# A state-space and attention kernel: VectorE exp rewritten and used in 96 bursts instead of 82, the skip product moved from TensorE to VectorE, the second state bank freed by row quarters

## Chip, cores, metric

One core of one Trainium2 chip. The metric is the device time of one execution in microseconds (us), the median of several runs. All runs quoted here were in the fast state, which means that none was over 1.5% above the fastest run of the same kernel. A ratio is the mean time of one kernel's fast runs over the mean of the other kernel's fast runs of the same rounds, so it is not quite the ratio of the medians that stand beside it.

In what follows PE is TensorE's matmuls and PEld its weight loads, DVE is VectorE, ACT is ScalarE, POOL is GpSimd, SP is SyncE, and a trailing q (SPq) is an engine's sequencer, which issues DMAs and waits. A line number such as L1085 is a line of that run's own kernel, so the same code has different numbers in different kernels.

## The reference

Two branches read the same `x` (2048 x 1024, bf16) and are mixed by a gate:

```python
g = sigmoid((x * gate_w).sum(-1, keepdims=True))
# a: a diagonal complex state-space layer
h = Lam_bar * h + (x @ B_bar.T)[t]          # along t, 1024 complex states
a = 2.0 * (hseq @ Cmat.T).real + x * Dskip  # x * Dskip is the "skip product"
# b: attention, 32 heads of 32, softmax over 2048 keys
p = softmax(q @ k.T * 32 ** -0.5); b = (p @ v) @ wo
return g * a + (1 - g) * b
```

## The kernel before

The attention is cut into 512 bursts (8 groups of four heads x 8 query blocks x 8 key blocks). A burst makes two tiles of scores, 128x1024 each, in PSUM, the memory that PE writes its results to. Three such tiles of PSUM rotate. ScalarE takes exp of a tile in one instruction. In some bursts ("VectorE bursts") the second half of the first tile, 128x512, goes to VectorE instead. In the gaps PE does everything else, in chains of matmuls into one PSUM bank: projections of the next head group, the state inputs ("u"), the state outputs ("c", 32 tiles of 128x512), and at the end the output product.

The VectorE burst is five instructions:

```python
self.S.op("act", lambda e: e.activation(t[:, 0, :], ps[:, 2 * s, :], ACT.Exp, scale=SCALE), ...)
self.S.op("dve", lambda e: e.tensor_scalar(xi, ps[:, 2 * s + 1, :], EXP_A, EXP_B, ALU.mult, ALU.add), ...)   # exp_a
self.dx += [... tensor_scalar(hi, hi, 0.0, 128.0, ALU.max, ALU.mult) ...,          # exp_b
            ... scalar_tensor_tensor(xw, lo, EXP_C2, lo, ALU.add, ALU.mult) ...,   # exp_c
            ... scalar_tensor_tensor(xw, xw, EXP_C1, lo, ...) ...,                 # exp_d
            ... scalar_tensor_tensor(t[:, 1, :], xw, EXP_C0, ev, ...) ...]         # exp_f
```

A c tile is 16 matmuls and four small ones for the skip product (`x` block times a diagonal of `Dskip`). VectorE scales the sum into one buffer, `Ag[:, 0]`, and the SP queue stores it:

```python
for q in range(4):
    mms.insert(5 * q + 3, (0, lambda e, f, l, ...: e.matmul(ps[:, 7, 128 * q:128 * (q + 1)],
        xT[:, dt, 128 * tt:128 * (tt + 1)], self.diagD[:, dt, :], start=False, stop=False), ...))
def evac():
    self.dve(lambda e: e.tensor_scalar(a, ps[:, 7, :], self.gcol[:, 0, tt:tt + 1], None, ALU.mult), [("bank", 7), "g0"], [at], "evac_c")
    self.dma(lambda e: e.dma_start(self.agd[tile], a), [at], [("agd", tile)], "st_a")
```

Nearly all DMAs are issued by SP, in the order in which a scheduler recorded them; a DMA that has to wait makes SP wait, and all behind it (7.42 us in the timeline below). What must be waited for is worked out from tokens: who writes a token waits for its last writer and readers. A head group's projection weights are three loads of 256 KB (`part` 1, 2, 0). From group 3 on, their buffer has also been scratch for VectorE bursts, so they write that scratch's tokens as well.

Of the kernel before, what the change touches and what calls it, by code (L numbers as in the profile page):

```python
# [8 lines left out]
I32 = mybir.dt.int32  # L9
# [15 lines left out]
RC_MIN = 1e-10  # L25
RC_MAX = 1e12
# [707 lines left out]
class GpPhaseA:  # L734
# [196 lines left out]
ACT_LAG = 0.466  # L931
# [7 lines left out]
EXP_A = 16713.9646930418  # L939
EXP_B = 4936176.0  # L940
EXP_C2 = 189883.03836007958
EXP_C1 = 38303098318.667244
EXP_C0 = 3607248267949745.0
# [3 lines left out]
    "u2 p2 u4 p1 u2 p2 u2 p9 u8 p1 u1 p1 u1 p1 u1 p1 u1 p1 u1 p1 u1 p1 c1 p2 c1 p2 c1 p1 u4 c1 u2 p1 c1 p2 c1 u2 p4 c1 p2 c1 u2 p3 u2 c2 u1 c6 u1 p12 u4 "  # L947
    "p1 u2 p1 u4 p9 c5 p1 c3 u4 p1 u2 p1 u2 p1 u4 p1 u2 p8 u2 p9 c8 p3 o36 ").split())
DVB_RUNS = ((109, 113), (129, 177), (185, 257), (277, 277), (285, 329), (345, 345), (365, 381), (389, 453), (461, 505))
# [19 lines left out]
class FastPath:  # L969

    def __init__(self, nc, S, es, d, flag):
# [20 lines left out]
        hp = T("hp", [128, 2, 8, 512], BF)  # L992
        self.hpb = [hp, self.OT[:, 4:8, :].rearrange("p (r a) n -> p r (a n)", r=2).rearrange("p r (j t) -> p r j t", j=8)]
# [14 lines left out]
        self.diagD = T("diagD", [128, 8, 128], BF)  # L1008
# [6 lines left out]
        self.badb = T("badb", [128, 2], BF)  # L1015

# [14 lines left out]
        hx = [hp[:, r, 4:8, :].rearrange("p a n -> p (a n)") for r in range(2)]  # L1031
        wx = [self.w[:, x].rearrange("p q a n -> p (q a n)") for x in range(2)]
        ag = self.Ag[:, 1, :]
        self.xt = half(wx[0]) + half(wx[1]) + half(hx[0]) + half(self.OT[:, 6, :]) + [ub[:, 0], ub[:, 1]]
        self.xi = [wx[0][:, 2048:3072], wx[1][:, 2048:3072], hx[1][:, 0:1024], self.OT[:, 7, 0:1024], self.ut[:, 0, :]]
        self.xi = [ap.bitcast(I32) for ap in self.xi]
        self.xw = [ag, ag, hx[1][:, 1024:2048].bitcast(F32), self.OT[:, 7, 1024:2048].bitcast(F32), self.ut[:, 1, :]]
# [56 lines left out]
    def begin(self):  # L1094
        S, d = self.S, self.d
        pool, dve, act = self.pool, self.dve, self.act
        warm = self.hpb[0][:, 0, 0, :]
# [61 lines left out]
    def opening(self):  # L1159
        S, ps, w, xT, dve = self.S, self.ps, self.w, self.xT, self.dve  # L1160

        def evac(dst, bank, tok, first, eng=dve):
            src = ps[:, bank, 0:256]
            kw = dict(reads=[("bank", bank)])
            kw.update(dict(writes=[tok]) if first else dict(acc=[tok]))
            if eng is dve:
                S.op("dve", lambda e: e.tensor_copy(dst, src), name="evac_qk", **kw)
            else:
                S.op("act", lambda e: e.activation(dst, src, ACT.Copy), name="evac_qk", **kw)
        for word in self.OPENING.split():  # L1170
# [44 lines left out]
            elif op == "M":  # L1215
# [7 lines left out]
                self.diag_d()  # L1223
# [86 lines left out]
    def diag_d(self):  # L1310
        for j in range(8):
            self.pool(lambda e, j=j: e.tensor_scalar(self.diagD[:, j, :], self.ident[:], self.pf[:, 3, j:j + 1], 0.0, ALU.mult, ALU.add),
                      ["ident", ("pf", 3)], [("diagD", j)])
# [36 lines left out]
    def item_ops(self, j, ch, n):  # L1350
        dve, ub, tq, ut, ht = self.dve, self.ub, self.tq, self.ut, self.ht
        b = self.hp_of[ch]
        hp = self.hpb[b]
        er, ei = self.Et[:, 0, j, :], self.Et[:, 1, j, :]
# [3 lines left out]
        t = [tq[:, i, :] for i in range(4)]  # L1358
        ops = []
# [17 lines left out]
        late = lambda: []  # L1377
        if ch == 2 and j >= 4:
            late = lambda: self.x_toks(2)
        if b == 1 and j == 0:  # L1380
            hw = ["fX", "fY", "m_c"] + self.EFtok + ["gp%d" % i for i in range(4)]
        tt(0.335, hp[:, 0, j, :], t[0], t[1], ALU.subtract, [("tq", 0)], lambda: [("hp", b, j, 0)] + hw + late())
        tt(0.335, hp[:, 1, j, :], t[2], t[3], ALU.add, [("tq", 2)], lambda: [("hp", b, j, 1)] + hw + late())
        if j == 7 and ch < 3:
            ops.append((0.0, self.carry))
        return ops

# [29 lines left out]
    def d_qk(self, g, part, ch, bank=7):  # L1417
        ps, w, xT = self.ps, self.w, self.xT
        mms = []
        for a in range(8):  # L1420
            mms.append((1, lambda e, f, l, a=a: e.matmul(ps[:, bank, :], w[:, g % 2, part, a, :], xT[:, a, 512 * ch:512 * (ch + 1)], start=f, stop=l),  # L1421
                        [("w", g % 2, part)] + self.xtok(ch)))
        if part == 0:
            z = (4 * g + ch) % 5
            dst, tok = self.Q[:, z, :], ("Q", z)
        else:
            dst, tok = self.K[:, g % 2, 512 * ch:512 * (ch + 1)], ("K", g % 2, ch)
        return self.chain(mms, "proj", lambda: self.dve(lambda e: e.tensor_copy(dst, ps[:, bank, :]), [("bank", bank)], [tok], "evac_qk"), bank)
# [42 lines left out]
    def d_c(self, ch, tq, cb, k):  # L1471
        ps, xT, cT = self.ps, self.xT, self.cT
        b = self.hp_of[ch]
        hp = self.hpb[b]
        tt = 4 * ch + tq
        cols = slice(128 * tq, 128 * (tq + 1))
        mms = []
        for j in range(8):
            for ri in range(2):
                mms.append((1, lambda e, f, l, j=j, ri=ri: e.matmul(ps[:, 7, :], hp[:, ri, j, cols], cT[ri][:, j, 512 * cb:512 * (cb + 1)], start=f, stop=l),  # L1480
                            [("hp", b, j, ri), ("cTf", ri, j)]))


        for q in range(4):
            dt = 4 * cb + q
            mms.insert(5 * q + 3, (0, lambda e, f, l, q=q, dt=dt: e.matmul(ps[:, 7, 128 * q:128 * (q + 1)], xT[:, dt, 128 * tt:128 * (tt + 1)], self.diagD[:, dt, :],  # L1486
                                                                          start=False, stop=False), [("diagD", dt)] + self.xtok(ch)))
# [4 lines left out]
        def evac():  # L1492
            self.dve(lambda e: e.tensor_scalar(a, ps[:, 7, :], self.gcol[:, 0, tt:tt + 1], None, ALU.mult), [("bank", 7), "g0"], [at], "evac_c")
            self.dma(lambda e: e.dma_start(self.agd[tile], a), [at], [("agd", tile)], "st_a")
# [4 lines left out]
    def ld_a(self, k):  # L1499

        tile = self.a_order[k]
        x = [("hp", 0, j, ri) for j in range(8) for ri in range(2)] if k == 0 else []
# [43 lines left out]
    def plan(self):  # L1546
# [5 lines left out]
        for B in range(NBURST):  # L1552
            for q in range(4):
                late = B in DVB and q == 1
                parts.append((B + 2 + (2 if late else 0), B, q))
# [59 lines left out]

    def x_set(self, B):

        g, pg = divmod(B, 64)
        if g == 7 or B >= 433:
            return 4  # L1620
        if pg < 52:
            return g % 2
        return 2 if g < 4 else 3

    def x_of(self, B, n):
        return len(self.tile) - 10 + 2 * self.x_set(B) + n

    def x_toks(self, k):
        t0 = len(self.tile) - 10 + 2 * k
        assert not any(self.left_in.get(t0 + t, 0) for t in range(2)), (self.p, k)  # L1630
        assert not self.dx or self.x_now != k
        return [(n, t0 + t) for n in ("pt", "ptd") for t in range(2)] + [("xi", k), ("xw", max(k, 1))]
# [24 lines left out]
    def exp(self, B, z, s):  # L1657
# [7 lines left out]
        else:  # L1665
            self.act(lambda e: e.activation(self.tile[p], ps[:, 2 * s:2 * s + 2, :], ACT.Exp, scale=SCALE), [("S", s)], [("pt", p)], "exp")  # L1666

    def dve_exp(self, B, s, p):
# [3 lines left out]
        halves = xi.bitcast(U16).rearrange("p (n two) -> p n two", two=2)  # L1672
        lo, hi = halves[:, :, 0], xi.bitcast(I16).rearrange("p (n two) -> p n two", two=2)[:, :, 1]
        ev = xi.bitcast(BF).rearrange("p (n two) -> p n two", two=2)[:, :, 1]
        deps = []
        use = (k, B // 64 if k < 2 else 0)
        self.x_now = k
        if use not in self.seen_x:
            self.seen_x.add(use)
            if k < 2:  # L1680
                assert self.busy_w != B // 64
                over = [("w", k, q) for q in range(3)] + [("Ag", 1)]
            elif k < 4:
                assert self.c_left[k - 2] == 0
                over = [("hp", k - 2, j, ri) for j in range(8) for ri in range(2)]
# [3 lines left out]
            for o in over:  # L1689
                deps += [self.S.tok_w.get(o)] + self.S.tok_r.get(o, [])  # L1690
        self.S.op("act", lambda e: e.activation(t[:, 0, :], ps[:, 2 * s, :], ACT.Exp, scale=SCALE), reads=[("S", s)], writes=[("pt", p)], deps=deps, name="exp")  # L1691
        self.S.op("dve", lambda e: e.tensor_scalar(xi, ps[:, 2 * s + 1, :], EXP_A, EXP_B, ALU.mult, ALU.add), reads=[("S", s)], writes=[("xi", k)], deps=deps, name="exp_a")  # L1692
        kw = max(k, 1)
        I, W = ("xi", k), ("xw", kw)
        assert not self.dx, (self.p, [c for c, _ in self.dx], self.log[-8:])
        self.waiting.add(B)
        self.last_dx, self.dx_due = True, B + 3
        self.dx += [(0.365, lambda: self.dve(lambda e: e.tensor_scalar(hi, hi, 0.0, 128.0, ALU.max, ALU.mult), [I], [I], "exp_b")),
                    (0.603, lambda: self.dve(lambda e: e.scalar_tensor_tensor(xw, lo, EXP_C2, lo, ALU.add, ALU.mult), [I], [W], "exp_c")),
                    (0.603, lambda: self.dve(lambda e: e.scalar_tensor_tensor(xw, xw, EXP_C1, lo, ALU.add, ALU.mult), [I, W], [W], "exp_d")),  # L1700
                    (0.603, lambda: self.dve(lambda e: e.scalar_tensor_tensor(t[:, 1, :], xw, EXP_C0, ev, ALU.add, ALU.mult), [I, W], [("ptd", p)], "exp_f")),  # L1701
                    (0.0, lambda: self.waiting.discard(B))]
# [29 lines left out]
    def normalize(self, U):  # L1732
# [8 lines left out]
        x = [("hp", 1, j, ri) for j in range(8) for ri in range(2)] if g >= 4 and qb == 0 else []  # L1741
        assert not x or self.c_left[1] == 0
# [5 lines left out]
        if qb == 0 and g >= 6:  # L1748
            assert all(self.x_set(B) != 3 or B < U * BURSTS for B in DVB)
            x += self.x_toks(3)  # L1750
# [5 lines left out]
    def build(self):  # L1756
# [28 lines left out]
        proj[0] = [self.d_qk(0, 0, 2), self.d_qk(0, 0, 3)]  # L1785
        us, cs = [], []
        for ch in range(4):
# [3 lines left out]
            for cb in range(2):  # L1791
                for tq in range(4):
                    cs.append((ch, self.d_c(ch, tq, cb, len(cs))))
        self.c_left = [8, 8, 8, 8]
# [21 lines left out]
        log = self.log = []  # L1816
        for p in range(first, NBURST):
# [9 lines left out]
            if isd:  # L1827
                self.dve_t = max(self.dve_t, T + QK_LAG) + 0.608
                ta = max(ta, self.dve_t + 0.19)
# [325 lines left out]
```

## Time and profile before

928.42 us, median of 4 runs (927.99 to 929.23). The profiled run's span is 926.5 us.

| | before |
|---|---|
| exp tiles of 128x1024 on ACT | 942 |
| exp halves of 128x512 on ACT (as many on DVE) | 82 |
| DVE busy | 737.3 us |
| granted TensorE clock | 0.998 |

The page's first part has, for each engine, the busy time, its share of the span and the number of instructions.

```profile
span 926.5 us, 33493 instructions
...
PE 892.4 (96%) x15095; PEld 525.4 (57%) x15316; DVE 737.3 (80%) x1331; ACT 911.3 (98%) x1034; POOL 8.9 (1%) x39
```

ACT at 98% could still be full of overlapping records, so one looks for its rhythm. The chain of waits of before, in order of time (start us, length us, what):

```profile
718.56 6.42 ACT f_pt L1666 x7
725.47 6.42 ACT f_pt L1666 x7
```

Seven full tiles take 6.42 us, 0.917 us each. The next seven start 6.91 us later; between them is one half tile, which so costs 0.49 us. 942 x 0.917 + 82 x 0.49 = 904 us of the 926.5 us.

The groups of instructions of before, by form: busy us, mean ns of one, idle time of the engine before them and what ended it.

```profile
L1666 ACT ACTIVATE f_pt<-f_ps 128x1024 bf16<-128x1024 f32 x862 | 814.2, 1209 | 0.6 <-PE f_ps L1650 0.6
...
L1692 DVE TENSOR_SCALAR f_wb<-f_ps 128x512 int32<-128x512 f32 x53 | 36.6, 691 | 52.4 <-PE f_ps L1650 52.3
L1701 DVE SCALAR_TENSOR_TENSOR f_wb<-f_Ag,f_wb 128x512 bf16<-128x512 f32 x53 | 36.5, 689 | 1.2
...
L1698 DVE TENSOR_SCALAR f_wb<-f_wb 128x512 int16<-128x512 int16 x53 | 23.8, 449 | 0.1
```

In this main group ACT waited 0.6 us in all for scores. The steps of a VectorE burst take 0.69 and 0.45 us. The other way round, PE waits for ACT; waits of before (us in total, times, longest us):

```profile
PEld f_ps L1650 <- ACT f_pt L1666: 63.4, 153, 0.6
```

Two stretches of before will matter later. Each row has the busy us (and instructions) of PE, PEld, DVE, ACT and POOL, then the granted clock, the DMA share and GB/s:

```profile
200.00:250.00 50.00, 49.06 (x821) 29.20 (x828) 45.72 (x81) 50.00 (x57) 0.00 (x0) 1.00 0.16 43
550.00:600.00 50.00, 48.92 (x804) 27.39 (x821) 30.44 (x57) 49.96 (x58) 0.00 (x0) 1.00 0.20 59
```

And one part of the timeline of before that I did not look at before predicting, the SP queue around the weight loads of group 3 (start us, us, what):

```profile
234.90 7.42 SPq L1079 DMA_DIRECT2D f_wb<-in_B_wqkv_dram  x3
242.37 1.54 SPq L1494 DMA_DIRECT2D ag_scratch<-f_Ag  x1
249.65 1.17 SPq L1751 DMA_TRANSPOSE f_OT<-f_On  x1
```

Three loads, each of which takes about 0.6 us to issue (e1 below), keep SP for 7.42 us, because each waits for the one before to land. I call this the hold. Behind it stands the store of a c tile. Nobody needed it soon.

I had a sign of the hold all the same. By the order of my queries, I asked for the table of SP's waits before I predicted, and it has this line (us in total, times, longest us):

```profile
SPq L1079 <- DMA f_wb<-in_B_wqkv_dram: 25.6, 10, 2.8
```

### The profile page before, as it was taken

The page shows a single profiled execution, that of the slowest core. Times are in us where ns is not written, and L with a number is a line of the kernel's source. Part 1 is how long each engine was busy: PE and PEld are TensorE (multiplying, and loading weights), DVE is VectorE, ACT ScalarE, POOL GpSimd, SP SyncE. Part 2 cuts the span into 40 slices and gives each one's busy share as a digit, 9 for nine tenths or more (in the row PEclk, how much of TensorE's full clock was granted, in tenths as well). Part 3 has the DMA queues.
Part 4 walks back from the last instruction along what each step waited for, and adds up shares of the span by engine and source line. Part 5 has one row for each costly group of instructions (what it writes and reads, how often), then busy time and mean ns, then how long its engine had stood idle before and what let it go on. Part 6 is the DMA issues. An engine that isn't in the chain of part 4 may idle for free.

```text
span 926.5 us, 33493 instructions
## 1 busy us (share of the span) xinstructions
PE 892.4 (96%) x15095; PEld 525.4 (57%) x15316; DVE 737.3 (80%) x1331; ACT 911.3 (98%) x1034; POOL 8.9 (1%) x39
## 2 busy tenths in 40 slices
PE   8899999999999999999999999999999999999996
PEld 4555755566555655555755755555565655555553
DVE  2799999999888888867889966679888765766775
ACT  6999999999999999999999999999999999999997
POOL 2000000000000000000000000000000000000000
PEclk9999999999999999999999999999999999999999
DMA  9649613210230113113033102133210111434322
GB/s 202 107 79 156 106 31 74 42 42 28 66 72 30 30 43 73 41 40 53 19 75 58 25 16 65 53 66 59 39 38 12 52 52 56 161 88 122 117 65 75
DMA packets 157076, 60.90 MB, mean 66 GB/s; under 512 B 145664, under 2 KB 145664, under 8 KB 156928
## 3 DMA queue, kind: packets, MB, share of 16 engines
q1 hardware_dynamic: 154768, 58.16, 28.3%
q8 instruction: 121, 1.98, 0.9%
q10 hardware_dynamic: 2160, 0.53, 0.3%
q14 instruction: 27, 0.22, 0.1%
HBM read 16.79 MB, written 12.58 MB: 32 GB/s over the span
## 4 chain that ended last, share of the span: by engine, by line
PE 55%; ACT 37%; DVE 5%; issue 1%; SPq 1%; DMA 1%; DVEq 0%
ACT f_pt L1666 33%; PE f_ps L1725 16%; PE f_ps L1650 11%; PE f_ps L1480 8%; PE f_ps L1451 8%; PE f_ps L1421 8%; PE f_ps L1439 4%; SPq L1074 1%; ACT f_ub L1691 1%; ACT f_wb L1691 1%; DVE f_ht L1370 1%; DMA f_xT<-in_A_x_dram 1%; ACT f_Et L1666 1%; ACT f_cT_re L1666 1%; PE f_ps L1486 1%
## 5 line engine op out<-in xcount | busy, mean ns | idle before, releaser
L1666 ACT ACTIVATE f_pt<-f_ps 128x1024 bf16<-128x1024 f32 x862 | 814.2, 1209 | 0.6 <-PE f_ps L1650 0.6
L1725 PEld LDWEIGHTS f_ps<-f_V,f_pt 128*128 128x128 bf16 x6896 | 239.4, 96 | 135.9 <-issue 96.9
L1725 PE MATMUL f_ps<-f_V,f_pt 128*128 128x33 bf16 x6896 | 293.0, 178 | 0.2 <-ACT f_pt L1666 0.2
L1650 PE MATMUL f_ps<-f_Q,f_K 32*128 32x256 bf16 x4096 | 220.9, 273 | 4.2 <-ACT f_pt L1666 1.2
L1650 PEld LDWEIGHTS f_ps<-f_Q,f_K 32*128 32x128 bf16 x4096 | 72.7, 92 | 118.4 <-ACT f_pt L1666 63.4
L1451 PE MATMUL f_ps<-f_xT,f_wb 128*128 128x512 bf16 x448 | 117.4, 377 | 8.2 <-issue 2.1
L1421 PE MATMUL f_ps<-f_xT,f_wb 128*128 128x512 bf16 x406 | 106.7, 378 | 4.5 <-issue 0.5
L1370 DVE TENSOR_TENSOR_SCAN f_ht<-f_pf,f_init,f_ut 128x512 bf16<-128x512 f32 x64 | 80.2, 1271 | 0.0
L1692 DVE TENSOR_SCALAR f_wb<-f_ps 128x512 int32<-128x512 f32 x53 | 36.6, 691 | 52.4 <-PE f_ps L1650 52.3
L1480 PE MATMUL f_ps<-f_cT_im,f_hp 128*128 128x512 bf16 x189 | 71.4, 378 | 3.0
L1511 PE MATMUL f_ps<-f_wb,f_OT 128*128 128x512 bf16 x218 | 57.8, 378 | 3.0 <-issue 0.2
L1451 PEld LDWEIGHTS f_ps<-f_xT,f_wb 128*128 128x128 bf16 x512 | 40.2, 96 | 33.4 <-issue 1.9
L1439 PE MATMUL f_ps<-f_wb,f_xT 128*128 128x128 bf16 x896 | 59.1, 219 | 0.0
L1480 PE MATMUL f_ps<-f_cT_re,f_hp 128*128 128x512 bf16 x147 | 55.5, 378 | 0.2
L1421 PEld LDWEIGHTS f_ps<-f_xT,f_wb 128*128 128x128 bf16 x464 | 36.2, 96 | 28.2 <-DVE f_ub L1457 0.3
L1439 PEld LDWEIGHTS f_ps<-f_wb,f_xT 128*128 128x128 bf16 x896 | 50.4, 97 | 0.0
L1457 DVE CAST f_ub<-f_ps 128x512 bf16<-128x512 f32 x48 | 33.0, 687 | 14.5 <-PE f_ps L1451 14.1
L1362 DVE TENSOR_TENSOR f_tq<-f_ht,f_Et 128x1024 bf16<-128x1024 bf16 x64 | 42.3, 684 | 0.4
L1362 DVE TENSOR_TENSOR f_ut<-f_tq 128x512 f32<-128x512 bf16 x64 | 42.3, 683 | 0.0
L1691 ACT ACTIVATE f_wb<-f_ps 128x512 bf16<-128x512 f32 x53 | 38.4, 725 | 0.1
L1701 DVE SCALAR_TENSOR_TENSOR f_wb<-f_Ag,f_wb 128x512 bf16<-128x512 f32 x53 | 36.5, 689 | 1.2
L1700 DVE SCALAR_TENSOR_TENSOR f_Ag<-f_Ag,f_wb 128x512 f32<-128x512 f32 x53 | 36.3, 685 | 0.7
(160 smaller groups left out, 925.4 us busy)
## 6 DMA issues: line engine op xcount, KB each, us to landing
ag_scratch<-f_Ag SPq DMA_DIRECT2D x32, 256.0 KB, 2.3
f_hp<-ag_scratch SPq DMA_DIRECT2D x32, 256.0 KB, 3.0
f_wb<-in_B_wqkv_dram SPq DMA_DIRECT2D x21, 256.0 KB, 3.5
out_dram<-f_xT SPq DMA_DIRECT2D x16, 256.0 KB, 2.1
f_wb<-in_B_wo_dram SPq DMA_DIRECT2D x1, 1024.0 KB, 6.2
f_OT<-f_On SPq DMA_TRANSPOSE x63, 2.4
f_wb<-in_B_wo_dram SPq DMA_DIRECT2D x1, 768.0 KB
f_wb<-in_B_wqkv_dram ACTq DMA_DIRECT2D x2, 256.0 KB, 4.1
```

The costliest lines, as they stand in the source:

```text
L1362: ops.append((c, lambda: dve(lambda e: e.tensor_tensor(o, a, b, op), r, w() if callable(w) else w)))
L1370: ops.append((1.192, lambda ri=ri: dve(lambda e: e.tensor_tensor_scan(ht[:, ri, :], rr, ut[:, ri, :], self.init[:, ri, j:j + 1], ALU.mult, ...
L1421: mms.append((1, lambda e, f, l, a=a: e.matmul(ps[:, bank, :], w[:, g % 2, part, a, :], xT[:, a, 512 * ch:512 * (ch + 1)], start=f, stop=l ...
L1439: m = e.matmul(ps[:, bank, 128 * q:128 * (q + 1)], xT[:, a, 128 * kt:128 * (kt + 1)], w[:, g % 2, 2, a, :], start=(a == 0), stop=(a == 7))
L1451: mms.append((1, lambda e, f, l, a=a: e.matmul(ps[:, 7, :], bT[:, n % 2, ri, a, :], xT[:, a, 512 * ch:512 * (ch + 1)], start=f, stop=l), [ ...
L1480: mms.append((1, lambda e, f, l, j=j, ri=ri: e.matmul(ps[:, 7, :], hp[:, ri, j, cols], cT[ri][:, j, 512 * cb:512 * (cb + 1)], start=f, sto ...
L1511: mms.append((1, lambda e, f, l, j=j: e.matmul(ps[:, 7, :], OT[:, j, 256 * qb + 128 * r:256 * qb + 128 * (r + 1)], wo[j][0][:, 512 * cb:51 ...
L1650: m = e.matmul(ps[:, 2 * sl[z] + h % 2, 256 * kl:256 * (kl + 1)], K[32 * h:32 * h + 32, g % 2, 128 * kt:128 * (kt + 1)], Q[32 * h:32 * h + ...
L1666: self.act(lambda e: e.activation(self.tile[p], ps[:, 2 * s:2 * s + 2, :], ACT.Exp, scale=SCALE), [("S", s)], [("pt", p)], "exp")
L1691: self.S.op("act", lambda e: e.activation(t[:, 0, :], ps[:, 2 * s, :], ACT.Exp, scale=SCALE), reads=[("S", s)], writes=[("pt", p)], deps=d ...
L1692: self.S.op("dve", lambda e: e.tensor_scalar(xi, ps[:, 2 * s + 1, :], EXP_A, EXP_B, ALU.mult, ALU.add), reads=[("S", s)], writes=[("xi", k ...
L1725: m = e.matmul(ps[:, 6, o:o + 33], self.tile[p][:, h2, 256 * kl + 128 * qt:256 * kl + 128 * (qt + 1)], V[:, g % 2, 2 * i + kl, h, :], star ...
```

## The change

Its intent is to take work from ScalarE. The exp on VectorE is rewritten to need four instructions: Q is scaled by 128 log2(e) when it is evicted, so a score is already a bf16 bit pattern up to a constant, and a cubic correction of the low bits is written as int16. All exps carry a factor of 2^65 that the softmax division removes. 14 more bursts use it, and the first comes at burst 65 instead of 109. To relieve PE the skip product goes to VectorE; for it, rows of `x` must be loaded again in their own layout (`ld_xn`, two loads of 64 KB for each c tile). The second state bank is freed by row quarters, which lets the order of c tiles change. The weight loads no longer write the token of the second scratch (`xw`), which lies beside their buffer. They still write the tokens of the scratch within it.

```diff
-DVB_RUNS = ((109, 113), (129, 177), (185, 257), ...)             # 82 bursts
+DVB_RUNS = ((65, 65), (70, 70), (73, 73), (84, 84), ...)         # 96 bursts
# ... ORDER, the sequence of u, p, c and o chains, is new as well
# evac_c and the load for the next c tile
-            self.dve(lambda e: e.tensor_scalar(a, ps[:, 7, :], self.gcol[:, 0, tt:tt + 1], None, ALU.mult), [("bank", 7), "g0"], [at], "evac_c")
-            self.dma(lambda e: e.dma_start(self.agd[tile], a), [at], [("agd", tile)], "st_a")
+            self.dve(lambda e: e.scalar_tensor_tensor(a, ps[:, 7, :], self.gcol[:, 0, tt:tt + 1], a, ALU.mult, ALU.add), [("bank", 7), "g0", ("Ag", 0, 1)], [at], "evac_c")
+            self.dma(lambda e: e.dma_start(self.agd[tile], a), [at, ("Ag", 0, 1)], [("agd", tile)], "st_a")
+            if self.c_next < 32:
+                self.ld_xn(*self.c_list[self.c_next])
# the skip product, two halves, into the same buffer as the eviction
+            ops.append((0.335, ... scalar_tensor_tensor(self.Ag[:, 0, 256 * k:256 * (k + 1)], self.xn[k], self.gcol[:, 0, tt:tt + 1],
+                                   self.drow[:, c0:c0 + 256], ALU.mult, ALU.mult) ...))
# the VectorE burst
-        self.S.op("act", ... ACT.Exp, scale=SCALE) ...
-        self.S.op("dve", ... tensor_scalar(xi, ps[:, 2 * s + 1, :], EXP_A, EXP_B, ALU.mult, ALU.add) ...
+        self.S.op("act", ... ACT.Exp, bias=OCTAVES * LN2, scale=LN2 / 128) ...
+        self.S.op("dve", ... tensor_scalar(xi, ps[:, 2 * s + 1, :], BITS_0, BITS_MIN, ALU.add, ALU.max) ...
-        # exp_b, exp_c, exp_d, exp_f
+        self.dx += [... scalar_tensor_tensor(xw, lo, 65536.0, lo, ALU.subtract, ALU.mult) ...,
+                    ... scalar_tensor_tensor(xw, lo, CUBE_C, xw, ALU.add, ALU.mult) ...,
+                    ... scalar_tensor_tensor(bits, xw, CUBE_K, xi, ALU.mult, ALU.add) ...]
# the tokens of the scratch that the weight loads write
-        return [(n, t0 + t) for n in ("pt", "ptd") for t in range(2)] + [("xi", k), ("xw", max(k, 1))]
+        return [(n, t0 + t) for n in ("pt", "ptd") for t in range(2)] + [("xi", k)] + ([("xw", k)] if k == 2 else [])
# ... cut: bank views by quarter, softmax range check, scheduler bookkeeping
```

## The prediction

> **What bounds the kernel now.** ScalarE. The engine table gives ACT 911.3 us of a 926.5 us span (98%), PE 892.4 (96%), DVE 737.3 (80%). The chain of waits from 597 us on is almost all ACT exp: 7 full tiles (128x1024) take 6.42 us, 0.917 us each, and 7 plus one half tile (128x512) repeat every 6.91 us, so a half tile costs 0.49 us. 942 full and 82 half tiles make 904 us. ACT runs without a hole from about 60 to 917 us. PE follows it: in the table of waits its score matmuls stand about 73 us for ACT to free a PSUM slot. So PE has slack, and DVE more.
>
> **What the change removes, adds and moves.**
>
> 1. Bursts with a half tile on VectorE: 82 -> 96. Each takes 0.917 - 0.49 = 0.427 us from ACT: 14 x 0.427 = 6.0 us, all on the bottleneck.
> 2. Such a half tile is five DVE instructions before (0.69 + 0.45 + 3 x 0.69 = 3.2 us by the groups), four after (about 2.75 us). 82 x 3.2 = 262 us becomes 96 x 2.75 = 264 us: fourteen more bursts for the same DVE time.
> 3. Exp gets a constant bias (2^65), in the built instruction an immediate, like the zero before. The Trainium skill, "ScalarE: Activation LUTs", "What ACT_TABLE_LOAD costs", has about 93 ns extra for each pointer operand, none for immediates: I expect 0.917 us again. This trace cannot show it.
> 4. The skip product leaves PE: 128 diagD matmuls, 55 ns start to start, 7 us. It comes to DVE as 64 products of 128x256, an estimate of 0.42 us each from the normalizing product of that width (0.424 us): 27 us, DVE to 765 us (83%). The eviction of c stays at 0.75 us, as the similar output eviction.
> 5. 64 more loads (4 MB of x) on the SP queue, and the second state bank freed by row quarter. DMA share is 20 to 30% in the middle; landing takes 2 to 3 us against about 7 us between c tiles. Off the critical path.
> 6. The first VectorE bursts move from burst 109 to 65, into 120 to 200 us, where windows show DVE 96% busy, and spacing becomes 3 to 5 instead of 4. A late first exp step there holds a PSUM slot, and ACT with it.
>
> **Critical.** Only point 1: -6 us. PE gains 7 us of room and the shorter ACT period takes 6 of it. Before, ACT lost about 9 us over the ideal sum (5 in the opening, 2.5 in the middle, 1.8 at the tail). For early VectorE bursts and skip products between their steps I allow 0.4 us more.
>
> **Predicted time:** 922.8 us (before 928.4), range 919.8 to 927.0. Faster by over 2%: 0.01; within 2%: 0.975; slower by over 2%: 0.015.
>
> **What would show it.** Right: 928 full exp tiles at 0.917 us and 96 half tiles at 0.49 us, ACT without a hole after 60 us and about 6 us less busy; no diagD matmuls; DVE near 765 us; PE still waiting tens of us for ACT. Wrong: exp over 0.917 us; ACT idle behind score matmuls that waited for DVE's first exp step, above all at 120 to 200 us; DVE idle before the skip product, released by a DMA; PE waiting for DVE's last exp step before value matmuls.
>
> **What would make it wrong.** DVE saturated at 120 to 200 us; the skip product stalling the in-order DVE for its load or for the store of the tile before; evictions late, and so PE. Also a failed range check at the end, which runs the slow general path.

## More of the kernel before

```python
def ld_w(self, g, part, eng="sp"):
    cb = 1024 * part + 128 * g
    self.dma(lambda e: e.dma_start(self.w[:, g % 2, part], self.wsrc[:, :, cb:cb + 128]), [],
             [("w", g % 2, part)] + (self.x_toks(g % 2) if g > 2 else []), "ld_w", eng)
# ...
if pg == (58 if g else 24) and g + 2 < GROUPS:     # pg: burst within the head group
    for part in (1, 2, 0):
        self.ld_w(g + 2, part)
```

Note that all three loads write the same scratch tokens. So the second waits for the landing of the first, and the third for that of the second.

## The result and the profile after

934.93 us (933.84 to 935.09, 4 runs) against 928.42 us; ratio 1.0067, 95% interval 1.0049 to 1.0084. The kernel is slower by 6.5 us, where 5.6 us of gain had been forecast.

```profile
span 932.1 us, 33379 instructions
...
PE 888.6 (95%) x14969; PEld 516.8 (55%) x15188; DVE 758.4 (81%) x1369; ACT 904.6 (97%) x1034; POOL 6.5 (1%) x31
```

ACT is busy 6.7 us less, and the span is 5.6 us longer. So ACT now has holes, stretches in which it stands. The groups of after:

```profile
L1691 ACT ACTIVATE f_pt<-f_ps 128x1024 bf16<-128x1024 f32 x848 | 801.7, 1138 | 7.3 <-PE f_ps L1675 7.1
...
L1714 ACT ACTIVATE f_wb<-f_ps 128x512 bf16<-128x512 f32 x77 | 53.4, 694 | 6.4 <-PE f_ps L1675 6.4
...
L1715 DVE TENSOR_SCALAR f_wb<-f_ps 128x512 f32<-128x512 f32 x77 | 52.8, 686 | 24.9 <-PE f_ps L1675 24.2
...
L1722 DVE SCALAR_TENSOR_TENSOR f_wb<-f_Ag,f_wb 128x512 int16<-128x512 f32 x77 | 52.7, 685 | 0.7
...
L1335 DVE SCALAR_TENSOR_TENSOR f_Ag<-f_xa,f_gcol,f_drow 128x256 f32<-128x256 bf16 x32 | 15.3, 479 | 12.5 <-DMA f_xa<-in_A_x_dram 12.5
L1335 DVE SCALAR_TENSOR_TENSOR f_Ag<-f_pf,f_gcol,f_drow 128x256 f32<-128x256 bf16 x32 | 15.3, 479 | 4.5 <-DMA f_pf<-in_A_x_dram 4.5
```

VectorE's steps take what was expected. ACT's records overlap, so their mean says little; its rhythm of full tiles is that of before:

```profile
460.74 6.42 ACT f_pt L1691 x7
```

The first two rows of the groups have ACT idle for 7.1 + 6.4 = 13.5 us for scores, where before it was 0.6 us. The last two are the skip product: 0.48 us each, and before it VectorE stood 12.5 + 4.5 us for the loads of `x`. The waits of after have the length of the worst ones:

```profile
DVE f_Ag L1335 <- DMA f_xa<-in_A_x_dram: 12.5, 9, 4.5
...
PE f_ps L1449 <- DVE f_Ag L1518: 9.6, 2, 5.0
...
ACT f_pt L1691 <- PE f_ps L1675: 7.1, 6, 5.2
ACT f_wb L1714 <- PE f_ps L1675: 6.4, 2, 5.6
```

Two waits of about 5 us on PE, behind the eviction of a c tile (L1518), and two of over 5 us on ACT. The windows say where; nearly all of ACT's loss is in these two:

```profile
200.00:250.00 50.00, 43.74 (x678) 23.42 (x687) 42.91 (x68) 44.77 (x51) 0.00 (x0) 0.95 0.34 77
550.00:600.00 50.00, 44.18 (x698) 23.64 (x709) 26.91 (x50) 43.72 (x51) 0.00 (x0) 0.93 0.21 61
```

ACT lost 5.2 and 6.3 us there. The chain of waits of after through the first hole:

```profile
234.19 3.08 DMA f_wb<-in_B_wqkv_dram
...
237.28 2.91 DMA f_wb<-in_B_wqkv_dram
...
240.21 0.37 SPq L1085
...
240.62 0.84 SPq L1519
...
241.50 2.57 DMA f_xa<-in_A_x_dram
...
244.09 0.88 DVE f_Ag L1335 x2
...
246.78 0.67 DVE f_Ag L1518
...
247.90 1.91 PE f_ps L1449 x4
```

Read it upwards: PE waits for bank 7, which the eviction of a c tile (L1518) frees; the eviction stands behind the skip product (L1335) on VectorE, which stood 4.47 us for the load with other work queued behind (1.8 us of state-space work, left out above, lies between the two); the skip product waits for a load of 64 KB; that load was issued at 241.50 because SP stood with the weight loads from 234.19 to 240.58. The same picture is at 574.8 us. The SP queue of after, in the order of issue:

```profile
234.19 6.39 SPq L1085 DMA_DIRECT2D f_wb<-in_B_wqkv_dram  x3
240.62 0.84 SPq L1519 DMA_DIRECT2D ag_scratch<-f_Ag  x1
241.50 0.43 SPq L1326 DMA_DIRECT2D f_xa<-in_A_x_dram  x1
```

The hold itself is not new: it was 7.42 us before. New is that something urgent stands behind it. The Trainium skill, "DMA: Bandwidth & Descriptors", "Anatomy of one DMA — SWDGE (gpsimd) path", says that DMA engines do not wait on semaphores and that a wait is made by the issuing sequencer before dispatch. That is what the timeline has: SP's entry of the three loads lasts 6.39 us, and the `x` load behind it was issued only at 241.50 us and then landed in 2.57 us. The section is written for loads issued by GpSimd; this shows it for loads issued by SP.

There is a second, smaller loss. The first four matmuls after the hole take 1.91 us in the chain's last row; elsewhere in the same chain four of that line take mostly 0.87 to 1.04 us. The Trainium skill, "TensorE: Matmul & The Clock Gate", "What's actually happening", has the clock at half after an idle window of about 3.4 us. PE stood 5.04 us here, and in windows of 2 us the granted clock is 0.50 from 246 to 252 us, where it was 1.00 up to 244 us; so far that fits. But in e1 below the clock also falls to 0.50 (246 to 248 us and 584 to 586 us) after PE stood only 1.51 and 1.57 us, and in e5 it stays at 1.00 after 1.94 us. So an idle window of 3.4 us is not what decided, and what did stays open.

The other three tied weight-load sets (at 353, 464 and 692 us) hold SP as long (7.04, 7.90 and 6.22 us). At 353 us the store and the `x` loads of a c tile stand behind them too. But the next skip product there comes at 385.8 us, and the one at 469.3 us has its loads from before the hold, so nothing waits.

### The profile page after: what moved, and what is told of

Same layout as the page of the kernel before. It is cut to its first block, busy times and chain, and to the rows that moved or that the text cites. A ratio compares the mean times of both kernels' runs of the same rounds, so it can differ in the third digit from the quotient of the medians.

```text
span 932.1 us, 33379 instructions
## 1 busy us (share of the span) xinstructions
PE 888.6 (95%) x14969; PEld 516.8 (55%) x15188; DVE 758.4 (81%) x1369; ACT 904.6 (97%) x1034; POOL 6.5 (1%) x31
## 4 chain that ended last, share of the span: by engine, by line
PE 49%; ACT 43%; DVE 3%; DMA 2%; issue 2%; SPq 0%; DVEq 0%
ACT f_pt L1691 38%; PE f_ps L1763 14%; PE f_ps L1675 10%; PE f_ps L1481 8%; PE f_ps L1449 8%; PE f_ps L1509 5%; PE f_ps L1469 4%; ACT f_wb L1714 2%; DMA f_wb<-in_B_wqkv_dram 1%; ACT f_ub L1714 1%; DMA f_xa<-in_A_x_dram 1%; ACT f_Et L1691 1%; ACT f_OT L1691 1%; ACT f_cT_re L1691 1%; PE f_ps L1132 1%
## 5 line engine op out<-in xcount | busy, mean ns | idle before, releaser
L1691 ACT ACTIVATE f_pt<-f_ps 128x1024 bf16<-128x1024 f32 x848 | 801.7, 1138 | 7.3 <-PE f_ps L1675 7.1
L1763 PEld LDWEIGHTS f_ps<-f_V,f_pt 128*128 128x128 bf16 x6784 | 235.3, 96 | 137.8 <-issue 88.8
L1763 PE MATMUL f_ps<-f_V,f_pt 128*128 128x33 bf16 x6784 | 288.6, 178 | 0.3
L1481 PE MATMUL f_ps<-f_xT,f_wb 128*128 128x512 bf16 x449 | 117.4, 377 | 7.2 <-issue 2.4
L1449 PE MATMUL f_ps<-f_xT,f_wb 128*128 128x512 bf16 x406 | 109.9, 387 | 13.9 <-DVE f_Ag L1518 9.6
L1715 DVE TENSOR_SCALAR f_wb<-f_ps 128x512 f32<-128x512 f32 x77 | 52.8, 686 | 24.9 <-PE f_ps L1675 24.2
L1714 ACT ACTIVATE f_wb<-f_ps 128x512 bf16<-128x512 f32 x77 | 53.4, 694 | 6.4 <-PE f_ps L1675 6.4
L1722 DVE SCALAR_TENSOR_TENSOR f_wb<-f_Ag,f_wb 128x512 int16<-128x512 f32 x77 | 52.7, 685 | 0.7
L1721 DVE SCALAR_TENSOR_TENSOR f_Ag<-f_wb,f_Ag 128x512 f32<-128x512 uint16 x77 | 52.7, 685 | 0.6
L1720 DVE SCALAR_TENSOR_TENSOR f_Ag<-f_wb 128x512 f32<-128x512 uint16 x77 | 52.7, 684 | 0.1
L1544 DVE SCALAR_TENSOR_TENSOR f_xT<-f_ps,f_gcol,f_hp 128x512 bf16<-128x512 f32 (+1 forms) x28 | 21.0, 751 | 26.6 <-PE f_ps L1538 26.6
```

The lines of the kernel that those rows point to most:

```text
L1449: mms.append((1, lambda e, f, l, a=a: e.matmul(ps[:, bank, :], w[:, g % 2, part, a, :], xT[:, a, 512 * ch:512 * (ch + 1)], start=f, stop=l ...
L1481: mms.append((1, lambda e, f, l, a=a: e.matmul(ps[:, 7, :], bT[:, n % 2, ri, a, :], xT[:, a, 512 * ch:512 * (ch + 1)], start=f, stop=l), [ ...
L1691: self.act(lambda e: e.activation(self.tile[p], ps[:, 2 * s:2 * s + 2, :], ACT.Exp, bias=OCTAVES * LN2, scale=LN2 / 128), [("S", s)], [("p ...
L1720: self.dx += [(0.603, lambda: self.dve(lambda e: e.scalar_tensor_tensor(xw, lo, 65536.0, lo, ALU.subtract, ALU.mult), [I], [W], "exp_b")), ...
L1763: m = e.matmul(ps[:, 6, o:o + 33], self.tile[p][:, h2, 256 * kl + 128 * qt:256 * kl + 128 * (qt + 1)], V[:, g % 2, 2 * i + kl, h, :], star ...
```

## The experiments

The theory, Q: the three weight loads wait for each other, SP waits with them for about 6 us, the loads of `x` and the store of the c tile stand behind them, and where c tiles follow each other this stops VectorE, then PE, then ScalarE. Rival D, the first thing that I had named as a danger: VectorE has too much work, or its early exp bursts come late. Rival B: it is the bytes of the weight loads in the DMA engines that delay the small loads, not the wait on SP.

### Each weight load names only its own scratch (e1)

Instruction order is the same on all engines; only waits go.

```diff
-  [("w", g % 2, part)] + (self.x_toks(g % 2) if g > 2 else [])
+  [("w", g % 2, part)] + (self.x_part(g % 2, part) if g > 2 else [])
+    def x_part(self, k, part):     # the scratch that lies in this third of the buffer
+        t0 = len(self.tile) - 6 + 2 * k
+        return [[(n, t0) for n in ("pt", "ptd")], [(n, t0 + 1) for n in ("pt", "ptd")], [("xi", k)]][part]
```

> The changed kernel with one edit: each of the three weight loads of a head group names only the exp scratch that lies in its own third of the buffer, so that they no longer wait for each other's landing; the order of the instructions on every engine is the same. Theory Q (the chained weight loads hold the in-order SP queue about 6 us, the x loads and the store of the c tile stand behind them, the skip product stalls VectorE, then PE, then ScalarE): the two holes of ScalarE of about 6 us at 240-250 and 579-590 us vanish, the weight loads are issued 0.6 us apart, and the time is 934.9 - 12.5 = about 922.4 us (920.5 to 924). Rival D (VectorE has too much work or its early exp bursts come late): no change, 934 to 935.5. Rival B (the weight loads' bytes delay the x loads in the DMA engines): the holes stay at about half, 928 to 933.

Measured: 925.15 us (924.73 to 928.55; the profiled run is the 928.55), ratio to before 0.9959 (0.9943 to 0.9976). The gain over the change is 9.8 us, not 12.5, and the time lies outside my range of 920.5 to 924 us. The holes shrink but stay. The trace is that of the slowest of the four runs, 3.4 us above the median, with a granted clock of 0.994 against 0.997 to 0.999 in the others; so the waits of the median run are probably shorter than those shown here. The SP queue:

```profile
235.65 1.93 SPq L1085 DMA_DIRECT2D f_wb<-in_B_wqkv_dram  x3
237.62 0.99 SPq L1519 DMA_DIRECT2D ag_scratch<-f_Ag  x1
238.65 0.43 SPq L1326 DMA_DIRECT2D f_xa<-in_A_x_dram  x1
```

Rival D is out: it expected no change. Of the 6.39 us hold, 1.93 us remain, the bare issue of three loads; then the store's issue takes 0.99 us (0.35 us elsewhere), and by the chain of that run the `x` load takes 3.49 us to land instead of 2.57. The last is a piece of rival B. In the waits of this run ACT still stands 3.4 + 3.0 us for scores, and about 3.5 us more than in e3 are left in the time.

### The same edit in the kernel before (e2)

> The same edit in the kernel before. Theory Q: the three weight loads there wait for each other too, but nothing urgent stands behind them in the queue, so the time stays at 928.4 +- 0.5 us though the loads now go out 0.6 us apart. If the chained loads cost by themselves (weights late for the projections), it would gain 1 us or more.

Measured: 929.01 us (928.78 to 929.12) against 928.62 us of its rounds, ratio 1.0001 (0.9985 to 1.0018). SP's entry of three loads shrinks from 7.42 to 2.56 us, and the time does not follow. As theory Q has it: the wait is harmless as long as nothing urgent is behind it.

### The tie kept, the loads issued two bursts apart (e3)

Only the order on SP differs from the changed kernel.

```diff
-                for part in (1, 2, 0):
-                    self.ld_w(g + 2, part)
+                self.w_due = [(p + 2 * n if g else p, g + 2, part) for n, part in enumerate((1, 2, 0))]
+            while self.w_due and self.w_due[0][0] <= p:
+                self.ld_w(*self.w_due.pop(0)[1:])
```

> The changed kernel with its original ties, but the three weight loads issued two bursts (about 3.6 us) apart instead of back to back, so that each finds the one before it landed. Only the order on the SP queue changes. Theory Q: the holes vanish, 922.4 us (920.5 to 924.5), as with the tie removed; the tie costs only because the queue waits in order. Rivals D: no change, 934 to 935.5. If the holes come from the tie in some way other than the queue (late weights), they stay.

Measured: 921.62 us (921.17 to 922.15), ratio 0.9921 (0.9905 to 0.9938): 13.3 us below the changed kernel and 7.0 us below the kernel before. A second set of five rounds gave 922.17 us against 929.11, ratio 0.9931 (0.9917 to 0.9944). The SP queue now lets the store and the `x` loads through between the weight loads:

```profile
233.93 0.57 SPq L1085 DMA_DIRECT2D f_wb<-in_B_wqkv_dram  x1
235.52 0.33 SPq L1519 DMA_DIRECT2D ag_scratch<-f_Ag  x1
235.88 0.43 SPq L1326 DMA_DIRECT2D f_xa<-in_A_x_dram  x1
236.36 0.46 SPq L1326 DMA_DIRECT2D f_pf<-in_A_x_dram  x1
237.12 3.47 SPq L1085 DMA_DIRECT2D f_wb<-in_B_wqkv_dram  x2
```

The waits of ACT in this run:

```profile
ACT f_pt L1691 <- PE f_ps L1675: 1.5, 4, 0.6
```

13.5 us have become 1.5 us. VectorE does the same work as in the changed kernel (757.9 us busy), which again speaks against rival D.

### The tie and the burst of loads kept, on GpSimd's queue (e7)

```diff
-                    self.ld_w(g + 2, part)
+                    self.ld_w(g + 2, part, "pool", 15)      # one semaphore of their own
```

> The changed kernel with its weight loads of head groups 2 to 7 issued on the GpSimd queue instead of SP's, still back to back and still each waiting for the landing of the one before. Theory Q (it is the in-order SP queue that passes the wait on to the x loads and the store): the holes vanish though the chain stays, 921.6 to 922.8 us. If the chained loads themselves (late weights, or bytes in the DMA engines at that moment) make the holes, they stay, 930 or more. The loads' landing times may differ on this queue.

Measured: 922.19 us (921.73 to 923.39), ratio 0.9933 (0.9916 to 0.9950). The chain is still there, now on POOL, and costs nothing:

```profile
225.78 0.91 POOL L1085 DMA_DIRECT2D f_wb<-in_B_wqkv_dram  x1 [44.18 <-PE f_ps L1763]
230.35 0.88 POOL L1085 DMA_DIRECT2D f_wb<-in_B_wqkv_dram  x1 [3.67 <-DMA f_wb<-in_B_wqkv_dram]
234.31 0.88 POOL L1085 DMA_DIRECT2D f_wb<-in_B_wqkv_dram  x1 [3.08 <-DMA f_wb<-in_B_wqkv_dram]
```

So it is neither late weights nor the chain as such; it is that the chain sat in the queue of the `x` loads and the store. A caveat: on POOL the loads also start earlier, at 225.8 us, so this run does not test the bytes at the same moment.

### The hold doubled with the same bytes (e8)

```diff
+        for lo, hi in ((0, 4), (4, 8)) if g > 2 else ((0, 8),):
+            self.dma(... self.w[:, g % 2, part, lo:hi], self.wsrc[:, lo:hi, cb:cb + 128] ..., "ld_w", eng)
```

> The changed kernel with each tied weight load cut in two, so that six loads wait for each other instead of three: the suspected hold of the SP queue, 6.2 us, becomes about 5 waits of 2.6 us, 12 to 14 us, with the same bytes. Theory Q: each of the two holes grows from about 6 to about 12 to 13 us, the other three weight loads still meet no c tile: 934.9 + 13 = about 948 us (943 to 953). Rival B (bytes) and rival D (VectorE's load): unchanged, 934 to 936.

Measured: 946.11 us (945.93 to 947.19), ratio 1.0191 (1.0174 to 1.0208), 11.2 us above the changed kernel. The hold is now

```profile
234.22 13.61 SPq L1086 DMA_DIRECT2D f_wb<-in_B_wqkv_dram  x6
```

and ACT's waits are

```profile
ACT f_wb L1715 <- PE f_ps L1676: 12.5, 2, 12.3
ACT f_pt L1692 <- PE f_ps L1676: 12.3, 6, 10.6
```

Hold and hole grow together: holds of 6.39 and 13.61 us in the first place, and 13.5 and 24.8 us of waiting in both together. The bytes are the same, so rival B cannot be the main cause.

### The skip product back on PE, tie kept (e5), and with spaced loads (e6)

The four diagonal matmuls come back, the `x` loads and skip instructions go; the places of everything else were held the same by keeping the scheduler's accounts.

```diff
+            mms.insert(5 * q + 3, (0, ... matmul(ps[:, 7, 128 * q:128 * (q + 1)], xT[...], self.diagD[:, dt, :], ...), ...))
-            self.dve(... scalar_tensor_tensor(a, ps[:, 7, :], gcol, a, ALU.mult, ALU.add) ..., "evac_c")
+            self.dve(... tensor_scalar(a, ps[:, 7, :], gcol, None, ALU.mult) ..., "evac_c")
-                self.ld_xn(*self.c_list[self.c_next])
```

> The changed kernel with the ties kept, but the skip product back as four matmuls per c tile and no x loads; the placement of all else is the same. Theory Q: without loads that VectorE waits for, no 6 us hole; the c tile's store still stands behind the weight loads, and the next eviction needs it only a tile later, so 922 to 925 us, of which at most 1.5 us is the store's. Rival D (VectorE's exp load or early bursts): stays near 935, less what 27 to 30 us of skip work on VectorE cost. If the holes stay in full with no x loads, theory Q is wrong about the x loads.

Measured: 930.72 us (928.79 to 931.94), ratio 1.0018 (1.0001 to 1.0036). My expectation of 922 to 925 us was a miss. Without `x` loads ACT still stands 4.0 + 1.9 us for scores, and the chain has another DMA in the first hole:

```profile
241.14 3.23 DMA ag_scratch<-f_Ag
...
244.46 0.76 DVE f_Ag L1525
```

This is the store of the c tile before: there is one buffer for c tiles, so the next eviction cannot write it until the store has landed, and the store stood behind the same weight loads. I had taken the store for harmless. So the hold blocks by two ways, the `x` load being the longer one. That this order of chains is exposed to it and the order of before is not can be read in the SP queue of before: the store held there to 242.37 us has no c tile close behind. In its other such place a store is held to 580.01 us, and the next eviction comes only at 587.49 us; stores land in 2.3 us (median of before).

> The spaced kernel with the skip product back on PE (four matmuls per c tile, no x loads), all else placed the same. The skip product was at no time on the bottleneck, so if moving it is worth nothing in itself: 921.6 +- 0.7 us. If PE's 7 us of room is needed at the shorter ScalarE period: 923 to 925 us, with ScalarE's spacing stretched in small pieces where c tiles run. The two holes of 2.5 and 4.3 us of the tied version with the skip on PE (their releaser was the store of the c tile, held behind the weight loads) must be gone in either case.

Measured: 924.60 us (923.87 to 925.00), ratio 0.9953 (0.9936 to 0.9970). The holes are gone. It is 3.0 us above e3 (by their ratios 0.9953 and 0.9921 of about 928.7 us) and 2.0 us above the second set of e3 (0.9931), so the skip product on VectorE is worth 2 to 3 us at this ScalarE period. That is little above the noise: each ratio is uncertain by about 1.6 us. ACT's busy time agrees, 907.4 us here and 904.2 us in e3 for the same 1024 exp tiles, without long waits, so the loss is in small stretches. PE's waits for ACT on the tiles of the main group fall from 62.3 us (e3) to 50.5 us: it has less room. That this is what costs the 2 to 3 us is argued, not shown.

### The first 14 VectorE bursts given back, spaced loads (e4)

The list of VectorE bursts without its first 14 (65 to 158), nothing else against e3.

> The changed kernel with the spaced weight loads, and with its first 14 VectorE bursts (bursts 65 to 158) given back to ScalarE, so 82 bursts as before. The spaced kernel took 921.6 us. If the gain of the change is the 14 half tiles taken from ScalarE, 14 x 0.427 = 6.0 us come back: 927.6 us (926.5 to 928.5). If the early bursts cost ScalarE something in the VectorE-bound stretch, less than 6.0 comes back; if they are worth nothing, 921.6.

Measured: 928.10 us (927.52 to 928.84), ratio 0.9996 (0.9979 to 1.0013). Against e3 that is 7.0 us by the ratios (0.9996 less 0.9921, of 928.7 us; 6.0 us against its second set), 6.3 us by the gaps of the medians to before of their own rounds, and 5.9 us by ACT's busy time (910.1 against 904.2 us). The forecast for the 14 bursts was 6.0. And these were the early ones, in the stretch that I had feared: no extra cost shows.

### The x loads issued ahead of the store (e9)

In e3 the skip product still waits for its load in some places, so I tried for more, with e3 again in the same rounds.

```diff
+        ops.append((0.0, lambda: self.c_next < 32 and self.ld_xn(*self.c_list[self.c_next])))   # after the skip product
-            if self.c_next < 32:
-                self.ld_xn(*self.c_list[self.c_next])                                         # was after the store
```

> The spaced kernel with each x load issued right after the skip products that free its buffer, ahead of the store of the c tile instead of behind it; compute engines' order unchanged. In the spaced kernel the skip product still waits 0.4 to 1.7 us for its x load in about ten places, and ScalarE loses about 2 us in the middle. If those waits are part of that loss: 920.3 to 921.2 us, half a us to one below the spaced kernel of the same rounds. If VectorE's waits there are covered by ScalarE's slack in PSUM: the same as the spaced kernel, within 0.5 us.

> The spaced kernel once more, for comparison on the same chip: 921.6 us (921.0 to 922.3).

Measured: 922.86 us (922.22 to 923.25), ratio 0.9935, against 922.17 us and 0.9931 for e3 again. No gain. VectorE's waits before the skip product fall from 10.0 us (e3) to 3.9 us, now for the store of the tile before, and the time does not follow: these short waits are covered by slack behind them. e3 has the lowest median that I measured; e7 and e9 are within the noise of it.

| version | us | ratio to before | ACT waiting for scores, us (main groups) |
|---|---|---|---|
| before | 928.42 | 1 | 0.6 |
| the change | 934.93 | 1.0067 | 7.1 + 6.4 |
| e8, hold doubled | 946.11 | 1.0191 | 12.3 + 12.5 |
| e5, skip on PE, tie kept | 930.72 | 1.0018 | 4.0 + 1.9 |
| e2, tie removed in before | 929.01 | 1.0001 | 0.6 |
| e4, 82 bursts, loads spaced | 928.10 | 0.9996 | 1.1 |
| e1, tie removed | 925.15 | 0.9959 | 3.4 + 3.0 |
| e6, skip on PE, loads spaced | 924.60 | 0.9953 | 0.6 |
| e9, x loads early, loads spaced | 922.86 | 0.9935 | 1.5 |
| e7, loads on POOL's queue | 922.19 | 0.9933 | 1.1 |
| e3, loads spaced | 921.62 | 0.9921 | 1.5 |

## Why the prediction was wrong

- **Point 5 is the step that failed**: "64 more loads (4 MB of x) on the SP queue ... landing takes 2 to 3 us against about 7 us between c tiles. Off the critical path." The landing time was right (2.57 us in the hole). What I left out is the time until the load is issued. SP waits in order, and twice it stood 6 us with weight loads that wait for each other, in front of an `x` load and a store that VectorE needed. That put 13.3 us into ScalarE's chain (the change against e3). It could have been read from the profile before: the SP queue shows one entry of three loads, 7.42 us long. I compared the DMA share and the landing time, which say nothing of a queue's waits. The table of SP's waits, which I had, does (25.6 us in 10 waits for weight loads), but the prediction makes nothing of it.
- Among the dangers I had named "the skip product stalling the in-order DVE for its load or for the store of the tile before". Both happened (the change, e5). I gave them 0.4 us together with the early bursts, and a 15-to-1000 chance of costing over 2%. Naming a wait without looking at the queue that serves it did not help.
- **Point 1 was right**: e4 against e3 gives 5.9 to 7.0 us for 14 bursts (with PE's room, see point 4); 6.0 were forecast. Full tiles stayed at 0.917 us.
- **Point 2 was right**: four steps of 0.685 us each instead of five.
- **Point 3 was right**: the runs of seven full tiles take 6.42 us after as before. The bias is an immediate, and the Trainium skill ("ScalarE: Activation LUTs", "What ACT_TABLE_LOAD costs") has extra time for pointer operands alone; the trace agrees for the immediate and has no pointer case.
- **Point 4 was half right**: the skip instruction takes 0.48 us, not 0.42, VectorE is busy 758 us, not 765. But "Critical. Only point 1" was not: without the skip product's move, e6 keeps 4.2 to 4.4 us of e3's 6.4 to 7.3. So the skip product's move is part of the gain at the shorter period, probably by the room that it leaves PE.
- **Point 6 was right to name and needless to fear**: ACT has no hole at 120 to 200 us, in any run.

Predicted with the hold left out: 922.8 us. Measured with the hold removed: 921.6 and 922.2 us. So the sum was right but for one term, which was missing.

What stays open: why e1, where the tie itself is gone, is about 3.5 us slower than e3. Its trace, that of its slowest run, has three terms (1.93 us of issue, the slower issue of the store, 0.9 us more to land) and a clock at half behind both holes, but no run takes them apart, and none tests the bytes alone at the same moment.

## What to carry to other kernels

A DMA queue that waits in order is an engine like any other: before you put a load on it that someone will wait for, read its timeline and look for entries that are much longer than their issue. A false dependence (here, the same tokens for three separate thirds of a buffer) can cost nothing in one version of a kernel (e2) and 13 us in the next, where something urgent is placed behind it; space such loads, split the token, or put them on another queue. And when a large change moves the time the wrong way while each instruction costs what it should, follow the chain through the largest hole before doubting the sums.

## What the Trainium skill lacked or had wrong

- "DMA: Bandwidth & Descriptors", "Issuing engines are not separate DMA queues", says that issuing on several engines only saves the sequencer's time to initiate, which is usually small. It lacks that a sequencer's semaphore waits are separated as well: moving 18 weight loads from SP to GpSimd took the kernel from 934.9 to 922.2 us, though the loads still waited for each other.
- The same page, under "Rules for kernel authors", has no warning of waits at the head of an in-order issuing queue. Here three chained loads held SP for 6.39 us (13.61 us when cut into six), and loads of 64 KB that land in 2.6 us stood behind them.
- No page seen gives the cost of a `scalar_tensor_tensor` of 128x256 in bf16 with a per-partition scalar and an f32 result: 0.479 us here, against 0.424 us for the normalizing product of that width that reads PSUM.
- "TensorE: Matmul & The Clock Gate", "What's actually happening", has half clock after an idle window of about 3.4 us. Here the granted clock was 0.50 also after PE stood 1.51 and 1.57 us (e1).
